# Turning the output projection on VectorE instead of folding it with an fp32 product, in a kernel of two attentions

## The chip, the cores and the metric

The kernel runs on one core of a Trainium2 chip. Its five engines have queues of their own: TensorE (PE in the profile; its weight loads are PEld), VectorE (DVE), ScalarE (ACT), GpSimd (POOL) and SyncE (SP), which here issues nearly all DMAs. They wait for each other by semaphores. The metric is the device time of one execution in microseconds; the median of several runs is compared.

## The reference, cut to what matters

Two attentions read the same input `x` (2048 tokens of 512), and a gate mixes them. Attention A is a recurrence over 64 segments of 32 tokens; each segment's input is 8 memory rows and its 32 tokens, and the first 8 rows of its output are the next segment's memory:

```python
g = sigmoid((x * gate_w).sum(-1, keepdims=True))
mem = mem0                                    # 8 rows of 512
for s in range(64):
    h = concatenate([mem, x[:, 32*s:32*s+32]])            # 40 rows
    q, k, v = h @ Wq, h @ Wk, h @ Wv                      # 32 heads of 128
    scores = where(mask, q @ k.T * scale, -1e9)           # memory rows see all keys, tokens causally
    o = (softmax(scores) @ v) @ Wo                        # back to 512, summed over the heads
    mem, out_a[s] = o[:8], o[8:]
# attention B: 32 heads of 16, four stretches of 512 tokens,
# causal softmax inside a stretch and a linear memory over the earlier ones
out = g * out_a + (1 - g) * out_b
```

All inputs are bf16.

## The kernel before, in words

**The two strands.** A's 64 segments (`p_seg`) are a chain: segment s+1 can't project before segment s has made its memory. B is cut into 16 units (`p_unit`: a stretch and 8 heads each), whose products fill TensorE's time while a segment waits. A third kind of filler are the "remainders": the last 8 tokens of each segment do not depend on the memory for their own projections, so `p_rest` projects those of four segments together, and a segment's own products have 32 rows (24 tokens and 8 memory rows).

**A segment.** The inputs of the projections are in `hT` (two buffers, 128 partitions x 4 chunks x 32 columns): 24 columns of tokens are copied from `xT` by GpSimd (L1441), 8 columns of memory come from the segment before. `wproj` (L1401) multiplies them with Wq, Wk and Wv, each product cut into four strips of 32 columns of the array (mode `c32`), four matmuls side by side. The results are copied out of PSUM to `st` (`copy`, L1001, on ScalarE or VectorE), transposed on VectorE to `KT` and `QT` (L1466), and multiplied to scores: first the mask as a product of `neg` and `hide` (`f_hide`, through `mm`, L1024), then the own scores (L1481) and those of the remainder's keys (L1485). ScalarE takes the exponential to `PT` (L1489); `ones` times `PT` gives the sums (L1504), ScalarE makes their reciprocal `rc` with a logarithm and an exponential (L1508, L1510), VectorE and GpSimd multiply `PT` with it (L1512, L1515), and TensorE multiplies with V (L1546, L1555, cut into strips of 32 rows, mode `r32`). The results are copied to `OT` (L1001), and `wo` multiplies them with Wo.

**`wo`.** 64 products a segment (L1300) leave four partial sums in one PSUM bank: partitions 0 to 63 hold the even heads, 64 to 127 the odd ones, and of each 64 the first 32 hold output columns 0 to 255 and the others 256 to 511, tokens along the partitions. The next segment needs the sum of the two halves, for the 8 memory rows, with the 512 columns along the partitions. The kernel before copies the bank to `part` in fp32 (name `par`), and multiplies each 128 columns of it with a fixed fp32 matrix `fold` of 16 columns, which picks the memory rows, adds the halves and turns the result (`f_fold`, through `mm`, L1024, in `c32`); VectorE copies the 32 columns to `hT` (name `hm`, L1323). The rows for the output are added from PSUM and `part` (name `row`, L1330) and go to DRAM (`a_rows`), from where `p_tail` reads them, scales them with the gate (L1275), adds B (L1283) and stores.

**B.** A piece of a unit is up to 16 `r32` products (L1141), two exponentials of 640 columns (L1159) and a causal select on GpSimd (L1165); pieces ride on a segment's PSUM banks (`carry`) or stand alone. Products with V are L1182, their transposes on VectorE L1218 and L1234. The gate itself is 64 products of one column (`f_gate`, L934), 16 for each 512 tokens.

**The start.** 16 MB of Wq, Wk, Wv and Wo are loaded in order by SP (`p_weight`, L897); before them come x and B's three projections (L806, 512 KB each), and small things, mem0 among them (L804).

**The order.** Every operation has a cost and a priority, and a planner (`schedule`) places operations on engines, modes and PSUM banks; but the sequence of each engine is not searched at build time: it is given by the text `ORDER`, which `sequences` unpacks. Costs only decide the engine's internal books. Each engine executes its sequence in that order and waits where a semaphore asks for it.

## Time and profile before

| | us |
|---|---|
| median of 3 runs | 830.68 (829.51 to 831.47) |
| profiled execution | 832.89 |
| its span, first to last instruction | 831.2 |
| TensorE busy | 809.5 (97%) |
| VectorE busy | 617.3 (74%) |
| ScalarE busy | 562.9 (68%) |
| GpSimd busy | 260.9 (31%) |
| granted TensorE clock | 0.998 |

Busy time counts any moment in which an instruction of the engine is under way. A matmul's record covers its way through the array, so that records overlap, and their sum says little; the chain of waits follows the work that ended last, from each step back to what released it, and gives every moment of the span to one step. Groups of instructions are listed as line, engine, operation, out<-in, shapes, count, then busy us, mean ns of one, and the engine's idle time just before them with what ended it.

### The profile page before, as it was taken

The numbers are of one execution on the slowest core, as the hardware profiler recorded it, in microseconds if no ns is written. First come the engines' busy times: TensorE is split into PE (matmuls) and PEld (weight loads), VectorE is DVE, ScalarE is ACT, GpSimd is POOL, SyncE is SP. The second block draws the span as 40 slices with busy tenths as digits, with TensorE's granted clock in tenths as the row PEclk, the third lists the DMA queues.
The fourth block names the chain that finished last, engine by engine and source line by source line (L and its number), as shares of the span: only waits on it lengthen the run. The fifth ranks groups of instructions, "written<-read, shape, count | busy, mean of one in ns | idle before, by whom it ended". The sixth has DMA issues, their size and how long they took to land.

```text
span 831.2 us, 53272 instructions
## 1 busy us (share of the span) xinstructions
PE 809.5 (97%) x24474; PEld 521.5 (63%) x24474; DVE 617.3 (74%) x1398; ACT 562.9 (68%) x1278; POOL 260.9 (31%) x576
## 2 busy tenths in 40 slices
PE   9999999999999999999999999999999999999987
PEld 4445666666666566666666666666766665666654
DVE  4688667768778768678676687776878767886776
ACT  3577676777766667776667766676656677767663
POOL 3443231323322332323233233423232223323340
PEclk9999999999999999999999999999999999999999
DMA  9983111121111111111011111100111100000001
GB/s 341 414 247 52 40 24 43 43 45 27 43 28 28 39 28 44 27 34 44 15 47 46 38 27 31 40 14 18 44 42 32 39 20 15 13 23 23 22 21 36
DMA packets 71701, 45.63 MB, mean 55 GB/s; under 512 B 50046, under 2 KB 69942, under 8 KB 69942
## 3 DMA queue, kind: packets, MB, share of 16 engines
q1 hardware_dynamic: 70422, 41.18, 17.5%
q8 instruction: 192, 3.15, 1.6%
...
q14 instruction: 31, 0.25, 0.1%
...
## 4 chain that ended last, share of the span: by engine, by line
PE 87%; DVE 4%; ACT 3%; DMA 2%; issue 1%; SPq 1%; POOL 0%; DVEq 0%; POOLq 0%
PE pb L1401 47%; PE pb L1300 17%; PE pb L1024 7%; PE pb L1141 4%; PE pb L1026 2%; PE pb L1546 2%; PE pb L1182 2%; DMA st<-in_A_mem_dram 2%; PE pb L1504 2%; PE pb L1481 1%; PE pb L1230 1%; PE pb L1555 1%; DVE KT_sb L1466 1%; PE pb L1485 1%; ACT rc_sb L1510 1%
## 5 line engine op out<-in xcount | busy, mean ns | idle before, releaser
L1001 ACT ACTIVATE st<-pb 128x512 bf16<-128x512 f32 (+2 forms) x313 | 149.0, 494 | 103.0 <-PE pb L1401 78.0
L1159 ACT ACTIVATE PTB<-pb 128x640 bf16<-128x640 f32 x240 | 158.4, 703 | 37.2 <-PE pb L1141 32.5
L1401 PE MATMUL pb<-Wv_sb,hT 128*32 128x512 bf16 x2048 | 162.8, 381 | 0.2 <-DVE ao L1330 0.2
L1401 PE MATMUL pb<-Wq_sb,hT 128*32 128x256 bf16 (+1 forms) x3072 | 138.0, 308 | 0.1
L1300 PE MATMUL pb<-Wo_sb,OT_sb 128*32 128x256 bf16 x4096 | 132.8, 273 | 3.0 <-issue 1.9
L1401 PE MATMUL pb<-Wk_sb,hT 128*32 128x512 bf16 x2048 | 132.0, 379 | 0.1
L1300 PEld LDWEIGHTS pb<-Wo_sb,OT_sb 128*32 128x32 bf16 x4096 | 100.7, 96 | 18.4 <-ACT OT_sb L1001 4.3
L1165 POOL TENSOR_SCALAR_AFFINE_SELECT PTB<-PTB 128x512 bf16<-128x512 bf16 x120 | 77.6, 647 | 107.4 <-ACT PTB L1159 100.8
L1515 POOL TENSOR_TENSOR PT_sb<-PT_sb,rc_sb 128x64 bf16<-128x64 bf16 x90 | 33.1, 367 | 248.9 <-ACT rc_sb L1510 240.5
L1401 PEld LDWEIGHTS pb<-Wq_sb,hT 128*32 128x32 bf16 x3072 | 82.5, 97 | 39.1 <-issue 0.8
L1466 DVE STREAM_TRANSPOSE QT_sb<-st 128x256 bf16<-128x256 bf16 (+1 forms) x192 | 94.4, 510 | 16.7 <-ACT st L1001 15.1
L1466 DVE STREAM_TRANSPOSE KT_sb<-st 128x512 bf16<-128x512 bf16 x128 | 89.4, 700 | 11.6 <-ACT st L1001 9.5
L1001 ACT ACTIVATE OT_sb<-pb 128x320 bf16<-128x320 f32 (+1 forms) x140 | 58.1, 428 | 37.9 <-PE pb L1555 36.3
L1401 PEld LDWEIGHTS pb<-Wk_sb,hT 128*32 128x32 bf16 x2048 | 57.0, 97 | 42.4 <-ACT PTB L1159 1.1
L1001 DVE CAST OT_sb<-pb 128x320 bf16<-128x320 f32 (+1 forms) x120 | 56.8, 478 | 31.3 <-PE pb L1555 29.3
L1401 PEld LDWEIGHTS pb<-Wv_sb,hT 128*32 128x32 bf16 x2048 | 52.2, 98 | 18.8 <-DVE ao L1330 0.7
L1508 ACT ACTIVATE rc_sb<-pb 128x160 f32<-128x160 f32 x128 | 38.8, 303 | 36.3 <-PE pb L1504 35.3
L1323 DVE CAST hT<-pb 128x32 bf16<-128x32 f32 x63 | 12.0, 191 | 66.4 <-PE pb L1024 66.1
L1489 ACT ACTIVATE PT_sb<-pb 128x224 bf16<-128x224 f32 x128 | 45.6, 356 | 17.4 <-PE pb L1485 12.8
L1001 DVE CAST V_sb<-pb 128x512 bf16<-128x512 f32 x65 | 44.5, 685 | 9.9 <-PE pb L1401 9.0
L1512 DVE TENSOR_TENSOR PT_sb<-PT_sb,rc_sb 128x160 bf16<-128x160 bf16 x128 | 42.7, 334 | 8.2 <-ACT rc_sb L1510 6.7
L1001 ACT ACTIVATE stg<-pb 128x512 bf16<-128x512 f32 (+1 forms) x68 | 37.9, 559 | 14.3 <-PE pb L1401 10.2
...
## 6 DMA issues: line engine op xcount, KB each, us to landing
...
```

Source lines behind the costliest of these rows:

```text
L1001: self.P.op(("act", "dve"), (lambda a: a.activation(dst, src(), ACT.Copy), lambda d: d.tensor_copy(dst, src())), reads=reads, writes=write ...
L1024: ins = pe.matmul(out[32 * c:32 * c + 32], lhsT[:, 32 * c:32 * c + 32], rhs, start=start, stop=stop, tile_position=(0, 32 * c), **kw)
L1141: ins = pe.matmul(pb[slot.banks[i]][:, base + a - lo:base + b - lo], KT[r0:r1, 128 * kc:128 * kc + 128], Q[r0:r1, t0 + a:t0 + b], start=Tr ...
L1159: P.op("act", (lambda dst=dst, src=src: lambda a: a.activation(dst, src(), ACT.Exp, scale=0.25))(), reads=[pair], writes=["%s%d_%d" % (nam ...
L1165: P.op("gp", (lambda pt=pt, ii=ii: (lambda g: g.affine_select(pt, pt, ([[0, len(ii)]] if len(ii) > 1 else []) + [[1, 128]], ALU.is_ge, 0.0 ...
L1300: ins = pe.matmul(pb[so.b][p0:p0 + 32, 0:256], tok(r, g, l), self.Wo[:, h, 256 * d:256 * d + 256], start=(r == 0 and g == 0 and l < 2), st ...
L1401: ins = pe.matmul(self.pb[sl.b][32 * g:32 * g + 32, 0:hi - lo], x[:, c, 0:32], cols, start=(c == 0), stop=(c == C - 1), tile_position=(0, ...
L1466: op("dve", (lambda dst=dst, src=src: lambda d: d.transpose(dst, src))(), reads=["st%d%s" % (i, tag)], writes=["%sT%d%s" % (kind, r, tag)] ...
L1489: op("act", lambda a: a.activation(PT[:, r, :], pb[rb.b][:, 0:224], ACT.Exp, scale=SCALE), reads=[rb], writes=["PT%d" % r, "PT%dr" % r], n ...
L1508: op("act", lambda a: a.activation(rc[:, r, :], pb[rb.b][:, 0:160], ACT.Ln), reads=[rb], writes=[rr], name="ln%d_%d" % (s, r), cost=t_act( ...
L1512: op("dve", lambda d: d.tensor_tensor(PT[:, r, 0:160], PT[:, r, 0:160], rc[:, r, :], ALU.mult), reads=[rp, rr], writes=[rp], name="nrm%d_% ...
L1515: op(("dve", "gp"), tuple((lambda e: e.tensor_tensor(rest, rest, late(rc[:, r, :]), ALU.mult)) for _ in range(2)), reads=[rp + "r", rr], w ...
```

## The change

- `wo`: the product with `fold` and the copy to `hT` go. VectorE transposes the PSUM bank's 256 fp32 columns in blocks of 32x32 to `rc` (`turn`), ScalarE or GpSimd moves the upper 64 partitions' memory columns to the lower 64 (`shift`), and two adds, on VectorE or GpSimd, put the sums of 64 partitions each into `hT` (`hm`). So that the blocks land where `hT` wants them, the products with Wo take 32 columns out of every 64 (`half`), and `p_tail` puts the columns back in order when it scales. The copy `par` is of the upper 64 partitions alone and has a later priority.
- The score bank is four pieces of 56 columns, 16 for the remainder and 40 of its own, instead of 160 and 64; the mask covers 40 of each, 160 columns instead of 224. What reads or writes scores and `PT` follows.
- The gate is made by 64 products of 128 columns in four column strips, with a transpose on VectorE behind each 16.
- B's first loads are of 384 columns instead of 512; the rest of them was not used from there.
- Costs and latencies of the planner are changed, and `ORDER` is new: all engines' sequences differ, the DMAs' too. In SP's, mem0 comes first.

The diff, without the two order texts, most changed costs and some renamings:

```diff
--- before
+++ after
@@ -13,71 +13,72 @@
 ORDER = (
...
@@ -658,7 +659,7 @@
         self.gB, self.omgB = self.rc[:, 1, 0:32], self.rc[:, 1, 32:64]
-        self.hide = t("hide_sb", [128, 224])
+        self.hide = t("hide_sb", [128, 160])
...
@@ -803,8 +803,8 @@
         for k in "kqv":
-            dma(self.g_wB[k], (lambda k: lambda s: s.dma_start(self.wB[k], self.B_w[k].rearrange("(c p) n -> p c n", p=128)))(k),
-                writes=["wB" + k], name="dma_wB" + k, prio=-102 if k == "k" else -99, load=dict(k=3.0, q=2.0, v=1.5)[k], cost=0.5, ring=4.0,
+            dma(self.g_wB[k], (lambda k: lambda s: s.dma_start(self.wB[k][:, :, 0:384], self.B_w[k].rearrange("(c p) n -> p c n", p=128)[:, :, 0:384]))(k),
+                writes=["wB" + k], name="dma_wB" + k, prio=-102 if k == "k" else -99, load=dict(k=2.7, q=1.6, v=1.15)[k], cost=0.5, ring=4.0,
...
@@ -820,9 +820,6 @@
         op("dve", lambda g: g.memset(self.MZf[:, :], 0.0), writes=["MZ16"], name="mz1", cost=0.15, prio=small)
-        for d in range(2):
-            op("dve", lambda v, d=d: v.tensor_tensor(self.fold[:, 8 * d:8 * d + 8], ident[:, 32 * d + 24:32 * d + 32], ident[:, 32 * d + 88:32 * d + 96],
-                                                     ALU.add), reads=["ident"], writes=["fold"], name="fold", cost=0.2, prio=small)
...
@@ -846,7 +843,8 @@
             op("dve", (lambda tile=tile: lambda g: g.memset(tile[:], 0.0))(), writes=[name], name=name + "0", cost=0.15, prio=small)
-        hide = [("hide", self.hide[0:32, lo:hi].rearrange("p (h q) -> p h q", h=4)) for lo, hi in ((0, 160), (160, 224))]
+        hide = self.hide[0:32, :].rearrange("p (h q) -> p h q", h=4)
+        hide = [("hide", hide[:, :, lo:hi]) for lo, hi in ((16, 40), (0, 16))]
...
@@ -929,14 +927,18 @@
             ins = None
-            for i in range(4):
-                for c in range(C):
-                    ins = pe.matmul(pb[sg.b][:, i:i + 1], xT[:, c, i * 128:(i + 1) * 128], self.gw[:, c:c + 1], start=(c == 0), stop=(c == C - 1))
+            for c in range(C):
+                part = xT[:, c, :].rearrange("p (i b t) -> p b i t", i=4, b=4)
+                for b in range(4):
+                    ins = pe.matmul(pb[sg.b][32 * b:32 * b + 32, 0:128], self.gw[:, c, :], part[:, b], start=(c == 0), stop=(c == C - 1),
+                                    tile_position=(0, 32 * b))
             return ins
-        P.op("pe", f_gate, reads=self.xres(sb) + ["gw"], writes=[sg], name="gate%d" % sb, cost=0.45, prio=prio + 0.1)
+        P.op("pe", f_gate, reads=self.xres(sb) + ["gw"], writes=[sg], name="gate%d" % sb, cost=0.23, prio=prio + 0.1, mode="c32")
         gs = self.g[:, 4 * sb:4 * sb + 4]
         rg, ro = "g%d" % sb, "omg%d" % sb
-        P.op("act", lambda a: a.activation(gs, pb[sg.b][:, 0:4], ACT.Exp, scale=-1.0), reads=[sg], writes=[rg], name="gate_e%d" % sb,
+        flat = self.adot[:, 0:8, :].rearrange("p a b -> p (a b)")
+        P.op("dve", lambda d: d.transpose(flat, pb[sg.b][:, 0:128]), reads=[sg], writes=["adot"], name="gate_t%d" % sb, cost=0.27, prio=prio + 0.1)
+        P.op("act", lambda a: a.activation(gs, flat.rearrange("p (i t) -> p i t", t=32)[:, :, 0], ACT.Exp, scale=-1.0), reads=["adot"], writes=[rg], name="gate_e%d" % sb,
...
@@ -1272,7 +1274,8 @@
               reads=["ad%d_%d" % (t, k) for k in range(n // 32)], writes=[ra], name="ain%d" % t, cost=0.4, load=0.2, prio=prio - 0.2)
-        P.op("dve", lambda d: d.tensor_scalar(self.t1[0:n, :], ain[0:n, :], self.g[0:n, t:t + 1], None, op0=ALU.mult),
+        P.op("dve", lambda d: d.tensor_scalar(self.t1[0:n, :].rearrange("p (m d i) -> p m d i", d=2, i=32), ain[0:n, :].rearrange("p (d m i) -> p m d i", d=2, i=32),
+                                             self.g[0:n, t:t + 1], None, op0=ALU.mult),
...
@@ -1289,6 +1292,11 @@
         so = P.slot("F", parts=True)
+
+        def half(h, d):
+            w = self.Wo[:, h, :]
+            return w[:, 256 * d:256 * d + 256] if late is None else w.rearrange("p (m d i) -> p d m i", d=2, i=32)[:, d]
+
...
@@ -1297,7 +1305,7 @@
                             p0 = 64 * q + 32 * d
-                            ins = pe.matmul(pb[so.b][p0:p0 + 32, 0:256], tok(r, g, l), self.Wo[:, h, 256 * d:256 * d + 256], start=(r == 0 and g == 0 and l < 2),
+                            ins = pe.matmul(pb[so.b][p0:p0 + 32, 0:256], tok(r, g, l), half(h, d), start=(r == 0 and g == 0 and l < 2),
...
@@ -1312,23 +1320,23 @@
         rhl = list(rhl) if isinstance(rhl, tuple) else [rhl]
-        self.copy(part, lambda: pb[so.b][:, 0:256], 256, [so], rhl, "par%s" % name, prio)
         if mem:
-            def f_fold(pe, m):
-                ins = None
-                for c in range(2):
-                    ins = self.mm(pe, m, pb[so.b][:, 256 + 16 * c:272 + 16 * c], part[:, 128 * c:128 * c + 128], self.fold[:, :], True, True)
-                return ins
-            P.op("pe", f_fold, reads=rhl + ["fold"], writes=[so], name="fold%s" % name, cost=0.15, prio=prio, mode=("c32",))
-            P.op("dve", lambda d: d.tensor_copy(mem[0].rearrange("p (d c) t -> p d c t", d=2),
-                                                pb[so.b][:, 256:288].rearrange("p (c d t) -> p d c t", c=2, d=2)), reads=[so], writes=[mem[1]],
-                 name="hm%s" % name, cost=0.19, prio=prio)
+            flat = self.rc[:, :, :].rearrange("p r x -> p (r x)")[:, 0:256]
+            turned = flat.rearrange("p (c e t) -> p e c t", c=4, e=2)
+            P.op("dve", lambda d: d.transpose(flat, pb[so.b][:, 0:256]), reads=[so], writes=["rc0", "rc1"], name="turn%s" % name, cost=0.43, prio=prio)
+            shift = self.rc[:, :, :].rearrange("p r x -> p (r x)")[0:64, 256:320].rearrange("p (e c t) -> p e c t", c=4, e=2)
+            P.op(("act", "gp"), ((lambda a: a.activation(shift, turned[64:128, :, :, 24:32], ACT.Copy)), (lambda g: g.tensor_copy(shift, turned[64:128, :, :, 24:32]))),
+                 reads=["rc0", "rc1"], writes=["rcs"], name="shift%s" % name, cost=(0.26, 0.26), prio=prio)
+            for e in range(2):
+                P.op(("dve", "gp"), tuple((lambda v, e=e: v.tensor_tensor(mem[0][64 * e:64 * e + 64], turned[0:64, e, :, 24:32], shift[:, e], ALU.add)) for _ in range(2)),
+                     reads=["rc0", "rc1", "rcs"], writes=["%s%d" % (mem[1], e)], name="hm%s_%d" % (name, e), cost=(0.16, 0.28), prio=prio)
+        self.copy(part[64:128, :], lambda: pb[so.b][64:128, 0:256], 256, [so], rhl, "par%s" % name, prio + 0.2 if mem else prio)
         i = self.__dict__.setdefault("nrow", [0])
         b = i[0] % 2
         i[0] += 1
         ao, rao = self.ao[b], "ao%d" % b
         P.op("dve", lambda d: d.tensor_tensor(ao[:, :], pb[so.b][0:64, 0:256], part[64:128, :], ALU.add), reads=[so] + rhl, writes=[rao],
-             name="row%s" % name, cost=0.45, prio=late)
+             name="row%s" % name, cost=0.42, prio=late)
...
@@ -1436,10 +1444,15 @@
             return P.slot("A")
+
+        def by_head(t):
+            return t.rearrange("p (l q) -> p l q", l=4)
+
+        mine, rest = [by_head(PT[:, r, :])[:, :, 16:56] for r in range(2)], [by_head(PT[:, r, :])[:, :, 0:16] for r in range(2)]
         xcol = (s % 16) * SEG
         xT = self.xT[sb % 2]
         op("gp", lambda g: g.tensor_copy(hv[:, :, 0:24], xT[:, :, xcol:xcol + 24]), reads=self.xres(sb, s % 16 // 4), writes=[rx],
-           name="hx%d" % s, cost=0.34, prio=s - 1)
+           name="hx%d" % s, cost=0.3, prio=s - 1)
...
@@ -1471,18 +1484,18 @@
             def f_hide(pe, m):
-                return self.mm(pe, m, pb[rb.b][:, 0:224], self.neg[:, :], self.hide[:, :], True, True, skip_group_check=True)
-            op("pe", f_hide, reads=["neg", "hide", "st%d" % i], writes=[rb], name="H%d_%d" % (s, r), cost=0.1, prio=prio, mode=FLEX)
+                return self.mm(pe, m, by_head(pb[rb.b][:, 0:224])[:, :, 0:40], self.neg[:, :], self.hide[:, :].rearrange("p (h q) -> p h q", h=4), True, True, skip_group_check=True)
+            op("pe", f_hide, reads=["neg", "hide", "st%d" % i], writes=[rb], name="H%d_%d" % (s, r), cost=0.072, prio=prio, mode=FLEX)
 
             def f_sc(pe):
                 ins = None
                 for l in range(4):
                     for g in range(4):
-                        ins = pe.matmul(pb[rb.b][32 * g:32 * g + 32, l * L:(l + 1) * L], KT[:, 16 * r + 4 * g + l, :], QT[:, 16 * r + 4 * g + l, :],
+                        ins = pe.matmul(pb[rb.b][32 * g:32 * g + 32, 56 * l + 16:56 * l + 56], KT[:, 16 * r + 4 * g + l, :], QT[:, 16 * r + 4 * g + l, :],
                                         start=False, stop=True, tile_position=(0, 32 * g), skip_group_check=True)
                 for g in range(4):
                     h0 = 16 * r + 4 * g
-                    ins = pe.matmul(pb[rb.b][32 * g:32 * g + 32, 160:224], Kr[:, h0:h0 + 4].rearrange("p h k -> p (h k)"), QT[:, h0:h0 + 4, 24:40],
+                    ins = pe.matmul(by_head(pb[rb.b][32 * g:32 * g + 32, 0:224])[:, :, 0:16], Kr[:, h0:h0 + 4].rearrange("p h k -> p (h k)"), QT[:, h0:h0 + 4, 24:40],
...
@@ -1500,7 +1513,7 @@
                     o = pb[rb.b][p0:p0 + n]
-                    for k, (dst, src) in enumerate(((o[:, 0:160], PT[:, r, 0:160]), (late(o[:, 0:160]), PT[:, r, 160:224]))):
+                    for k, (dst, src) in enumerate(((by_head(o[:, 0:160]), mine[r]), (late(o[:, 0:160]), rest[r]))):
...
@@ -1509,11 +1522,10 @@
                cost=0.335, prio=prio)
-            op("dve", lambda d: d.tensor_tensor(PT[:, r, 0:160], PT[:, r, 0:160], rc[:, r, :], ALU.mult), reads=[rp, rr],
-               writes=[rp], name="nrm%d_%d" % (s, r), cost=0.335, prio=prio)
-            rest = PT[:, r, 160:224].rearrange("p (l q) -> p l q", q=16)
-            op(("dve", "gp"), tuple((lambda e: e.tensor_tensor(rest, rest, late(rc[:, r, :]), ALU.mult)) for _ in range(2)), reads=[rp + "r", rr],
-               writes=[rp + "r"], name="nrr%d_%d" % (s, r), cost=(0.235, 0.33), prio=prio)
+            op("dve", lambda d: d.tensor_tensor(mine[r], mine[r], by_head(rc[:, r, :]), ALU.mult), reads=[rp, rr],
+               writes=[rp], name="nrm%d_%d" % (s, r), cost=0.345, prio=prio)
+            op(("dve", "gp"), tuple((lambda e: e.tensor_tensor(rest[r], rest[r], late(rc[:, r, :]), ALU.mult)) for _ in range(2)), reads=[rp + "r", rr],
+               writes=[rp + "r"], name="nrr%d_%d" % (s, r), cost=(0.3, 0.38), prio=prio)
...
@@ -1552,11 +1564,11 @@
                     o = pb[quad.banks[g]][:, 0:160].rearrange("p (l q) -> p l q", q=L)[:, :, 24:40]
-                    ins = pe.matmul(o, Vr[p0:p0 + 32, 128 * r:128 * r + 128], PT[p0:p0 + 32, r, 160:224],
+                    ins = pe.matmul(o, Vr[p0:p0 + 32, 128 * r:128 * r + 128], rest[r][p0:p0 + 32],
                                     start=False, stop=True, tile_position=(p0, 0), skip_group_check=True)
                 return ins
-            op("pe", f_pv, reads=["V%d" % r, "PT%d" % r], writes=quad.pairs + (self.early(3) if s == 0 else []), name="PV%d_%d" % (s, r), cost=0.11, prio=pPV[r], mode="r32")
-            op("pe", f_pw, reads=["PT%dr" % r, rVr[r]], writes=quad.pairs, name="PW%d_%d" % (s, r), cost=0.035, prio=pPV[r], mode="r32")
+            op("pe", f_pv, reads=["V%d" % r, "PT%d" % r], writes=quad.pairs + (self.early(3) if s == 0 else []), name="PV%d_%d" % (s, r), cost=0.088, prio=pPV[r], mode="r32")
+            op("pe", f_pw, reads=["PT%dr" % r, rVr[r]], writes=quad.pairs, name="PW%d_%d" % (s, r), cost=0.06, prio=pPV[r], mode="r32")
...
```

160 lines of the change are left out of this document (80 added, 80 removed).

## The prediction

> **What bounds the kernel now.** I read the page first: the engines' shares, then the chain that ended last.
>
> ```profile
> span 831.2 us, 53272 instructions
> PE 809.5 (97%) x24474; PEld 521.5 (63%) x24474; DVE 617.3 (74%) x1398; ACT 562.9 (68%) x1278; POOL 260.9 (31%) x576
> PE 87%; DVE 4%; ACT 3%; DMA 2%; issue 1%; SPq 1%; POOL 0%; DVEq 0%; POOLq 0%
> PE pb L1401 47%; PE pb L1300 17%; PE pb L1024 7%; PE pb L1141 4%; PE pb L1026 2%; PE pb L1546 2%; PE pb L1182 2%; DMA st<-in_A_mem_dram 2%; PE pb L1504 2%; PE pb L1481 1%; PE pb L1230 1%; PE pb L1555 1%; DVE KT_sb L1466 1%; PE pb L1485 1%; ACT rc_sb L1510 1%
> ```
>
> TensorE carries 87% of the chain and VectorE only 4%: what leaves TensorE's queue is worth nearly its own length, and what is added to VectorE is free as long as it ends before TensorE asks for it. TensorE's own length must not be read from the durations of single products, because these overlap. The chain between 400 and 430 us, one steady stretch of two to three segments, gives what each kind takes of the path (start, us, what):
>
> ```profile
> 404.79 0.43 PE pb L1401 x8
> 405.22 0.11 PE pb L1024 x16
> 405.58 4.01 PE pb L1401 x88
> 409.59 0.10 PE pb L1024 x4
> 409.68 0.22 PE pb L1401 x4
> 410.00 0.04 PE pb L1485 x4
> 411.00 0.10 PE pb L1504 x8
> 414.72 0.04 PE pb L1555 x4
> 417.48 0.11 PE pb L1024 x16
> ```
>
> Four 512-column products, one for each 32-column strip of the array, take 0.22 us together: 0.43 ns a column of such a set. There is no idle time to speak of between rows. The x16 rows of L1024 are the fp32 products (fold, eight products that the trace records as sixteen); the x4 row at 409.59 is the 224-column mask.
>
> **Fold out of TensorE.** 63 segments have one. On the chain it costs 0.11 us: 63 x 0.11 = 6.9 us, the lower end. The group that holds all of them, and the weight loads of the same product:
>
> ```profile
> L1024 PE MATMUL pb<-fold_sb,st 128*32 128x16 f32 x1008 | 19.9, 186 | 1.6 <-ACT st L1001 1.2
> L1024 PEld LDWEIGHTS pb<-fold_sb,st 128*32 128x32 f32 x1008 | 16.0, 110 | 13.4 <-ACT st L1001 8.7 <-DVE st L1001 1.9 <-issue 0.4
> ```
>
> 19.9 us of busy time is the upper end. The Trainium skill (Trainium Kernel Development and Optimization, Performance Expectations) says that busy time of matmuls is a bad measure because they are pipelined; these rows agree, 186 ns for one against 0.11 us for sixteen; by the rule the 19.9 is left aside, by busy time the sum below would be 11.4 us better. I take the chain's 6.9 and the 1.6 us that TensorE stood idle in front of fold: 8.5 us off.
>
> **What replaces it.** The old way from Wo's last product to the next segment's memory columns, once in full:
>
> ```profile
> 404.40 0.42 DVE L1001 COPY st<-pb 128x256 f32<-128x256 f32 x1 [2.50 <-PE pb L1300]
> 404.88 0.35 PEld L1024 LDWEIGHTS pb<-fold_sb,st 128*32 128x32 f32 x16 [0.16 <-DVE st L1001]
> 405.05 0.28 PE L1024 MATMUL pb<-fold_sb,st 128*32 128x16 f32 x16
> 405.43 0.19 DVE L1323 CAST hT<-pb 128x32 bf16<-128x32 f32 x1 [0.60 <-PE pb L1024]
> 405.68 0.60 PEld L1401 LDWEIGHTS pb<-Wq_sb,hT 128*32 128x32 bf16 x16
> ```
>
> From the copy's start to the first projection: 405.68 - 404.40 = 1.28 us. The new way has a 128x256 fp32 transpose out of PSUM, a 64x64 move of the upper partitions to the lower (48 on ScalarE, 15 on GpSimd in the new order), and two 64x32 adds, 115 of 126 on VectorE. None is in the trace; the nearest rows:
>
> ```profile
> L1466 DVE STREAM_TRANSPOSE QT_sb<-st 128x256 bf16<-128x256 bf16 x128 | 50.6, 415 | 4.1 <-ACT st L1001 3.4
> L1466 DVE STREAM_TRANSPOSE KT_sb<-st 128x512 bf16<-128x512 bf16 x128 | 89.4, 700 | 11.6 <-ACT st L1001 9.5
> L1218 DVE STREAM_TRANSPOSE t_sb<-pb 128x512 f32<-128x512 f32 x32 | 22.6, 706 | 2.5 <-PE pb L1182 2.5
> L939 ACT ACTIVATE g_sb<-pb 128x4 f32<-128x4 f32 x4 | 0.7, 173 | 0.5 <-PE pb L934 0.5
> L1508 ACT ACTIVATE rc_sb<-pb 128x160 f32<-128x160 f32 x128 | 38.8, 303 | 36.3 <-PE pb L1504 35.3
> L1108 DVE TENSOR_TENSOR MZ<-MZ,t_sb 128x17 f32<-128x17 f32 x12 | 2.0, 164 | 0.2
> L1515 DVE TENSOR_TENSOR PT_sb<-PT_sb,rc_sb 128x64 bf16<-128x64 bf16 x38 | 9.1, 240 | 2.2 <-ACT rc_sb L1510 1.8
> L1323 DVE CAST hT<-pb 128x32 bf16<-128x32 f32 x63 | 12.0, 191 | 66.4 <-PE pb L1024 66.1
> ```
>
> fp32 from PSUM costs a transpose nothing at 512 columns (706 against 700), so 0.42 us at 256. The move lies between 0.17 (4 columns) and 0.30 (160): 0.23. An add lies between 0.16 and 0.24: 0.18. A hand-over between engines is 0.06 (0.42 after 404.40, then 404.88). Quiet, the new way is 0.42 + 0.06 + 0.23 + 0.06 + 2 x 0.18 + 0.06 = 1.19 us (1.09 to 1.38 by the ends), against 1.28: no longer than the old one. It must be covered by products that need neither. I counted those between Wo's last product and the first projection in both instruction orders, at 0.43 ns a column: 1.17 us on average in the old, without fold, 1.24 in the new. Fold's own 0.11 was cover too, which makes 1.28 against 1.24. So the path gets hardly longer or barer, and I put this at 0; by the ends it is -0.19 + 0.04 = -0.15 to 0.10 + 0.04 = +0.14 us a segment, 9 us either way. An add that waits for the move holds up what the new order queues behind it on VectorE, the copy of the sums, the row's add and the next K and Q transposes, and the last of these wait for the projections anyway. The copy of the sums stays, on 64 partitions, and is put behind the memory columns, where only the row's way to DRAM waits for it.
>
> VectorE gains 63 x 0.42 + 115 x 0.18 - 12.0 = 35 us, and about 10 us of copies that the new order gives to it: 617 + 45 = 662 us, 81% of the new span. It stays below TensorE, with less slack for anything queued there.
>
> **Mask.** 64 columns fewer, 128 times (two a segment), at 0.43 ns: 3.5 us off; bounds 0 (if the x4 row's 0.10 were a floor) and 3.5. The price is a score bank in four pieces of 56, so that the mask, and the remainder's scores, are written in pieces. The softmax weights' products on VectorE and GpSimd read pieces too; they are off the path.
>
> **Gate.** Its 64 one-column products become 64 of 128 columns on four strips:
>
> ```profile
> L934 PE MATMUL pb<-gw_sb,xT 128*128 128x1 bf16 x64 | 2.2, 164 | 0.0
> L1401 PE MATMUL pb<-Wv_sb,hT 128*32 128x512 bf16 x2048 | 162.8, 381 | 0.2 <-DVE ao L1330 0.2
> L1401 PE MATMUL pb<-Wk_sb,hT 128*32 128x512 bf16 x2048 | 132.0, 379 | 0.1
> ```
>
> 2.2 us become 16 sets of 128 columns, 16 x 128 x 0.43 ns = 0.9 us: 1.3 off, with four small transposes beside it. Wo's weights are now read 32 columns out of every 64. That costs nothing: Wk is read in pieces of 32 already, Wv in one piece, 379 against 381 ns.
>
> **First loads.** Three of 512 KB lose a quarter, 384 KB in all, and mem0, on the chain with 14.39 us, goes to the head of SP's queue, past x, two of the three loads and Wv, which its 8 KB hardly delay.
>
> ```profile
> GB/s 341 414 247 52 40 24 43 43 45 27 43 28 28 39 28 44 27 34 44 15 47 46 38 27 31 40 14 18 44 42 32 39 20 15 13 23 23 22 21 36
> 7.18 14.39 DMA st<-in_A_mem_dram
> ```
>
> At 414 GB/s 384 KB are 0.9 us, by which the weights queued behind land earlier. The 14.39 us are no gain of that size: the first projection then waits for its weights, which come in that same stream. I take 0.9; bounds 0 and 3.
>
> **New order.** The other queues are shuffled throughout; in the two orders TensorE changes between products cut by rows and all others about equally often (372 and 370 times). I take 0. DVE, ACT, DMA, issue and SP hold 11% of the chain, 91 us; a tenth of it either way, 9 us, is the bound.
>
> **Sum.** 8.5 + 3.5 + 1.3 + 0.9 = 14.2 us off. The profiled execution took 832.9 us (its span and 1.7 us around it), 2.2 over the median of 830.7: 832.9 - 14.2 = 818.7 for its like, 816.5 for a median.
>
> **Rivals.** What a measurement of this kernel can tell from no change is about 0.2%, 1.7 us.
>
> (a) Fold's place becomes a wait. What counts for it: 13.4 us of idle weight loading stand ahead of fold, so TensorE does wait for this way today; the projection would wait in its stead. Then the 8.5 stay and 5.7 us go: 825.0.
>
> (b) The new order is better than the old by its bound, and takes another 9 us out of the 91: 807.5. For it: a little more cover (1.24 against 1.17); against it: nothing in the profile says that the remaining waits are needless.
>
> (c) Slower: the move waits on ScalarE. In the new order 44 of the 48 ScalarE moves stand right behind a half-unit exponential of
>
> ```profile
> L1159 ACT ACTIVATE PTB<-pb 128x640 bf16<-128x640 f32 x240 | 158.4, 703 | 37.2 <-PE pb L1141 32.5 <-DVE OT_sb L1001 3.2
> ```
>
> 0.70 us. One that starts with the transpose ends 0.28 us after it, one that starts at its end 0.70: 0.49 on average, and 44 x 0.49 = 21.6 us. That makes 816.5 + 21.6 = 838.1. It decides from 14.2 / 44 = 0.32 us a segment. Against it: ScalarE is idle 32% of the time, and the exponential may have run before Wo ends.
>
> (d) Writing in pieces slows the products: were the mask's 0.07 us (160 columns) and the remainder's 0.04 doubled, 128 x 0.11 = 14.1 us would come back and the time would be 830.6, no change. Against it: L1555 writes pieces of 16 out of 40 today and takes 0.04 us for four products of 64 columns, as L1485 does in one piece; that speaks plainly, so it gets little. The Trainium skill (SBUF — State Buffer, in the passage on cachelines under the DMA port swizzle) has the rule: any non-contiguous access to PSUM slows matmuls significantly. This trace disagrees at pieces of 16.
>
> **How the numbers follow.** Forecast 0.48; (a) 0.17; (b) 0.17; (c) 0.13; (d) 0.05. The likeliest gives 816.5, by its own bounds (9 us either way) 808 to 825. The range runs from 802 (a few us beyond b, since fold's true share may reach its upper end) to 831, which holds all but (c) and the far end of (b). Faster: forecast, a and b, 0.82, less a little for their tails: 0.80. Same: d, 0.05. Slower: c and tails, 0.15.
>
> **What would show it.** Right: no fp32 product in the groups, the mask's row at 0.07 us, TensorE's busy time down by some 14 us at the same 97%, VectorE near 81%, and the first projections of a segment released at about the old distance from Wo's end. Wrong: idle TensorE time in front of the projections put down to VectorE's adds or ScalarE's move (a, c), more than 0.04 us for the remainder's scores (d), or other waits that grew by more than 9 us in all.

## The result, and the profile after

The changed kernel takes 841.16 us (median of 4 runs, 840.17 to 842.98) against 831.08 us for the kernel before beside it (4 runs, 829.51 to 833.61): a ratio of 1.0121, 95% interval 1.009 to 1.0152. The forecast was 816.5 us, with a range from 802 to 831. The profiled execution took 840.17 us, with a span of 838.4.

The page of the changed kernel: its span, the engines' shares, and the chain that ended last, by engine and by line.

```profile
span 838.4 us, 51578 instructions
PE 804.2 (96%) x23514; PEld 497.5 (59%) x23514; DVE 669.8 (80%) x1556; ACT 565.5 (67%) x1286; POOL 269.2 (32%) x601
PE 73%; DVE 13%; ACT 4%; DMA 3%; issue 3%; SPq 2%; POOL 1%; DVEq 0%; POOLq 0%; ACTq 0%
PE pb L1409 40%; PE pb L1308 15%; PE pb L1026 5%; PE pb L1143 3%; PE pb L1558 2%; PE pb L1028 2%; PE pb L1184 2%; DVE rc_sb L1326 2%; DVE hT L1331 2%; PE pb L1494 2%; PE pb L1517 2%; DMA st<-in_gate_w_dram 1%; DVE stg L1003 1%; SPq L1381 1%; DVE ao L1338 1%
```

TensorE fell from 87% to 73% of the chain and VectorE rose from 4% to 13%. TensorE's busy time hardly moved (809.5 to 804.2 us); VectorE's grew by 52.5 us (617.3 to 669.8). The new operations are lines L1326 (turn), L1328 (move) and L1331 (adds). Groups of instructions, with mean duration in ns and the idle time ahead of them:

```profile
L1326 DVE STREAM_TRANSPOSE rc_sb<-pb 128x256 f32<-128x256 f32 x63 | 28.2, 448 | 45.0 <-PE pb L1308 44.6
L1328 ACT ACTIVATE rc_sb<-rc_sb 64x64 f32<-64x64 f32 x48 | 12.2, 254 | 26.5 <-DVE rc_sb L1326 26.1
L1331 DVE TENSOR_TENSOR hT<-rc_sb 64x32 bf16<-64x32 f32 x115 | 26.5, 231 | 14.1 <-ACT rc_sb L1328 8.5 <-POOL rc_sb L1328 3.1
L1026 PE MATMUL pb<-hide_sb,neg_sb 128*32 128x160 bf16 x508 | 31.6, 233 | 0.1
L1498 PE MATMUL pb<-QT_sb,rem_k 128*32 128x64 bf16 x512 | 27.1, 196 | 0.0
```

Beside its 54.7 us of turns and adds, VectorE stands idle for 14.1 us in front of adds, mostly because the move isn't done: an engine works in its given order, and what is queued behind an add waits too. One such way in the timeline, with nothing in between:

```profile
592.69 0.45 DVE L1326 STREAM_TRANSPOSE rc_sb<-pb 128x256 f32<-128x256 f32 x1 [0.92 <-PE pb L1308]
593.18 0.26 ACT L1328 ACTIVATE rc_sb<-rc_sb 64x64 f32<-64x64 f32 x1 [0.31 <-DVE rc_sb L1326]
593.47 0.40 DVE L1331 TENSOR_TENSOR hT<-rc_sb 64x32 bf16<-64x32 f32 x2 [0.32 <-ACT rc_sb L1328]
593.92 0.34 PEld L1409 LDWEIGHTS pb<-Wq_sb,hT 128*32 128x32 bf16 x12
```

From turn to projection that is 1.23 us, close to the 1.19 forecast. TensorE now waits for the adds and, for its PSUM banks, for the rows' adds (waits: us in total, times, longest):

```profile
PEld pb L1409 <- DVE hT L1331: 15.4, 32, 1.2
PE pb L1409 <- DVE hT L1331: 6.5, 20, 0.7
PEld pb L1409 <- DVE ao L1338: 5.8, 15, 1.0
```

In the kernel before, the same pairs stand at 1.1 us (hT) and 0.9 us (ao) on weight loading. Not all of the 15.4 us is new: there TensorE waited in front of fold instead, with the 13.4 us of idle weight loading that the prediction shows.

### The profile page after: what moved, and what is told of

It reads as the page before. It is cut to its first block, busy times and chain, and to the rows that moved or that the text cites. A ratio compares the mean times of both kernels' runs of the same rounds, so it can differ in the third digit from the quotient of the medians.

```text
span 838.4 us, 51578 instructions
## 1 busy us (share of the span) xinstructions
PE 804.2 (96%) x23514; PEld 497.5 (59%) x23514; DVE 669.8 (80%) x1556; ACT 565.5 (67%) x1286; POOL 269.2 (32%) x601
## 4 chain that ended last, share of the span: by engine, by line
PE 73%; DVE 13%; ACT 4%; DMA 3%; issue 3%; SPq 2%; POOL 1%; DVEq 0%; POOLq 0%; ACTq 0%
PE pb L1409 40%; PE pb L1308 15%; PE pb L1026 5%; PE pb L1143 3%; PE pb L1558 2%; PE pb L1028 2%; PE pb L1184 2%; DVE rc_sb L1326 2%; DVE hT L1331 2%; PE pb L1494 2%; PE pb L1517 2%; DMA st<-in_gate_w_dram 1%; DVE stg L1003 1%; SPq L1381 1%; DVE ao L1338 1%
## 5 line engine op out<-in xcount | busy, mean ns | idle before, releaser
L1003 ACT ACTIVATE st<-pb 128x512 bf16<-128x512 f32 (+2 forms) x286 | 140.0, 507 | 92.8 <-PE pb L1409 82.2
L1409 PE MATMUL pb<-Wv_sb,hT 128*32 128x512 bf16 x2048 | 158.4, 380 | 0.5 <-DVE QT L1001 0.3
L1308 PE MATMUL pb<-Wo_sb,OT_sb 128*32 128x256 bf16 x4096 | 136.2, 274 | 3.5 <-issue 2.3
L1308 PEld LDWEIGHTS pb<-Wo_sb,OT_sb 128*32 128x32 bf16 x4096 | 98.3, 96 | 24.0 <-ACT OT_sb L1003 4.8
L1409 PEld LDWEIGHTS pb<-Wq_sb,hT 128*32 128x32 bf16 x3072 | 79.9, 97 | 50.8 <-DVE hT L1331 4.9
L1479 DVE STREAM_TRANSPOSE KT_sb<-st 128x512 bf16<-128x512 bf16 x128 | 88.9, 697 | 15.2 <-ACT st L1003 13.4
L1003 ACT ACTIVATE OT_sb<-pb 128x320 bf16<-128x320 f32 (+2 forms) x133 | 54.8, 427 | 46.9 <-PE pb L1567 44.3
L1409 PEld LDWEIGHTS pb<-Wk_sb,hT 128*32 128x32 bf16 x2048 | 54.5, 96 | 53.6 <-DVE hT L1331 10.4
L1003 DVE CAST OT_sb<-pb 128x320 bf16<-128x320 f32 (+2 forms) x127 | 59.3, 478 | 24.0 <-PE pb L1567 23.0
L1326 DVE STREAM_TRANSPOSE rc_sb<-pb 128x256 f32<-128x256 f32 x63 | 28.2, 448 | 45.0 <-PE pb L1308 44.6
L1525 DVE TENSOR_TENSOR PT_sb<-PT_sb,rc_sb 128x160 bf16<-128x160 bf16 x128 | 42.8, 335 | 9.9 <-ACT rc_sb L1523 8.9
L1523 ACT ACTIVATE rc_sb<-rc_sb 128x160 f32<-128x160 f32 x128 | 43.0, 336 | 3.7 <-ACT rc_sb L1521 0.3
```

Of the source, the lines that this page charges most:

```text
L1003: self.P.op(("act", "dve"), (lambda a: a.activation(dst, src(), ACT.Copy), lambda d: d.tensor_copy(dst, src())), reads=reads, writes=write ...
L1308: ins = pe.matmul(pb[so.b][p0:p0 + 32, 0:256], tok(r, g, l), half(h, d), start=(r == 0 and g == 0 and l < 2), stop=(r == 1 and g == 3 and ...
L1326: P.op("dve", lambda d: d.transpose(flat, pb[so.b][:, 0:256]), reads=[so], writes=["rc0", "rc1"], name="turn%s" % name, cost=0.43, prio=prio)
L1409: ins = pe.matmul(self.pb[sl.b][32 * g:32 * g + 32, 0:hi - lo], x[:, c, 0:32], cols, start=(c == 0), stop=(c == C - 1), tile_position=(0, ...
L1479: op("dve", (lambda dst=dst, src=src: lambda d: d.transpose(dst, src))(), reads=["st%d%s" % (i, tag)], writes=["%sT%d%s" % (kind, r, tag)] ...
L1523: op("act", lambda a: a.activation(rc[:, r, :], rc[:, r, :], ACT.Exp, scale=-1.0), reads=[rr], writes=[rr], name="rc%d_%d" % (s, r), cost= ...
```

## The experiments

Four theories: the path (the way from Wo to the next segment's memory columns got longer), the order (the new sequences lose), the layout (operands in pieces are slow), and, from the second round on, VectorE's load (work on VectorE costs time wherever it stands). Names with b keep the old order, names with a the new one. Ratios are to the kernel before, run on the same chip, with a 95% interval in brackets; 0.1% is 0.83 us, and differences in us are worked out from the ratios. The kernels for which an operation had to be put into an order that was not made for it have it placed by hand, by the planned times.

### First round: which part of the change loses

**b_mask.** `ORDER` of before; mask, scores and loads of after.

> The kernel before, in its own order of instructions, with the 160-column mask, the new layout of the scores and the shorter first loads; the fold, the gate and the output rows stay as they were. Three theories for the 10.1 us that the whole change costs (841.2 against 831.1). Path: the turn, the move and the two adds are a longer way to the next segment's first operand than copy, fold and copy. Order: the edits are worth what they were thought to be, and the new order of the instructions loses more than that. Layout: operands read in pieces (scores, weighed values, Wo) are slower at TensorE or VectorE. Path and order expect 825 to 829 us here (3.5 us for the mask, 0.9 for the loads, up to 2 less); layout expects 835 us or more.

Measured: 829.78 us, ratio 0.9975 (0.995 to 0.9999). The layout does not lose; mask and loads bring about 2 us, only just clear of nothing. It is the fastest version here that computes everything, and the only one ahead of both kernels.

**b_turn.** The fold's part of `wo` is replaced as in the change's diff, with `half` for Wo; the rest is before.

> The kernel before, in its own order, with one edit: the fold and its two neighbours are replaced by the turn (at the old copy's time on VectorE), the move on ScalarE, the two adds on VectorE (right behind the move by the planned times) and the halved copy behind them; Wo is read in blocks of 32 columns with it. Every other instruction keeps its place. Path expects the whole loss here: 838 to 846 us. Order expects a gain or nothing: 822 to 831 us. Layout expects a small loss from Wo's pieces: 832 to 835 us.

Measured: 850.52 us, 1.0218 (1.0188 to 1.0249). The loss comes with the turn, and in the old order it is larger than the whole change's, and larger than path expected.

**a_fold.** The reverse: copy, fold and copy put into the changed kernel.

> The changed kernel in its own order, with the fold back: the turn, move and adds go; the copy of all 128 rows stands where the turn was (on the engine that had it in the kernel before), the fold is put on TensorE 0.62 us behind it by the planned times, and its copy on VectorE behind that. Mask, gate, loads and the order of all else are the changed kernel's. Path expects the loss gone: 826 to 832 us. Order expects it kept or grown, since the fold was fitted into this order by hand: 838 to 850 us.

Measured: 850.0 us, 1.0217 (1.0191 to 1.0242). Path expected the loss gone, and it grew. Taken with b_turn this decides nothing: each of the two operations was put by hand into an order that was made for the other, and both kernels are slow.

**b_all.** b_mask and b_turn together.

> The kernel before in its own order with the mask, the layout of the scores, the shorter loads and the turn together (all of the change but the gate's product and the new order). If the order alone loses: 819 to 828 us, the sum of the gains without the new order. If the path loses: 835 to 842 us, the path's loss less 4 us for mask and loads. Layout expects 838 us or more, and more than the turn alone.

Measured: 846.64 us, 1.0177 (1.0147 to 1.0207): b_turn less about 3.4 us, where mask and loads alone brought 2.1: the parts add up within their intervals. It is above the 835 to 842 that path expected, and layout, which expected more than for the turn alone, falls.

### Second round: path against load

**b_hm2.** Before, with `hm` (L1323) cut in two:

```diff
-P.op("dve", copy mem[0] <- pb[so.b][:, 256:288], name="hm")
+for e in range(2):
+    P.op("dve", copy mem[0][64*e:64*e+64] <- pb[so.b][64*e:64*e+64, 256:288], name="hm_e")
```

> The kernel before with one edit that makes its way from Wo to the next segment longer by a known piece and changes nothing else: the copy of the memory columns to hT is done in two halves of 64 partitions, one behind the other on VectorE, which adds about 0.19 + 0.03 = 0.22 us a segment to that way and 12 us of busy time to VectorE. Path theory (what counts is when the next segment's memory columns are ready): in the trace of before the projection starts some 0.09 us later than it could in the median segment, so that 0.13 to 0.22 us a segment come out at the end: 8 to 14 us, 839 to 845. Theory of VectorE's load: 12 us of 617 more, 831 to 834.

Measured: 838.57 us, 1.0092 (1.0068 to 1.0116), 7.6 us. The path theory holds for this edit: 63 x 0.22 = 13.9 us of path cost a little over half of that, just under the 8 to 14 expected. The second copy is VectorE work too, some 12 us.

**b_load.** Before, with two transposes whose results nobody reads:

```diff
 P.op("dve", ..., name="hm%s" % name)
+P.op("dve", transpose(spare, OT[:, 0:256]), name="duma%s" % name)
 P.op("dve", ..., name="row%s" % name)
+P.op("dve", transpose(spare, OT[:, 0:256]), name="dumb%s" % name)
```

> The kernel before with VectorE's load of the changed kernel and without its path: two transposes of 128x256 (0.42 us each, 52 us in all, as much as the change adds) whose results nobody reads, one right behind the copy of the memory columns, one right behind the output row's add. Path theory: 831 to 834 us, since both stand behind what the next segment waits for. Theory of VectorE's load (copies, transposes and sums that queue on a VectorE at 80% come late to TensorE): the loss comes here, 838 to 845 us.

Measured: 839.52 us, 1.0106 (1.0069 to 1.0143), 8.8 us. The load theory's case, off the path. The two groups, and the chain by engine:

```profile
L1334 DVE STREAM_TRANSPOSE spare<-OT_sb 128x256 bf16<-128x256 bf16 x63 | 28.1, 445 | 1.9
L1326 DVE STREAM_TRANSPOSE spare<-OT_sb 128x256 bf16<-128x256 bf16 x63 | 27.4, 435 | 0.1
PE 82%; DVE 8%; ACT 4%; DMA 3%; issue 2%; SPq 1%; POOL 0%; DVEq 0%; POOLq 0%
```

55.5 us of idle work on an engine that had 4% of the chain cost 8.8 us, 0.16 us each, and VectorE's share of the chain doubled. (The two rows add to 55.5 us, but the records of neighbours on VectorE overlap: its busy time on the page grew by 34.0 us, from 617.3 to 651.3, and by that the price is 0.26.) More waits of TensorE than before end with K's and Q's transposes and with the rows' adds:

```profile
PEld pb L1484 <- DVE QT_sb L1469: 7.2, 23, 0.7
PEld pb L1484 <- DVE KT_sb L1469: 4.9, 14, 0.5
PEld pb L1404 <- DVE ao L1331: 4.6, 16, 0.9
```

These were 4.1, 1.9 and 0.9 us.

**a_noshift.** The changed kernel without the move; `hm` adds `turned[0:64]` to itself.

> The changed kernel in its own order without the move between partitions: the two adds take the lower half twice, so the odd heads' half is left out of the memory rows. The way from Wo to hT is shorter by the move and its hand-over, 0.25 + 0.03 us quiet and more where it queues. Path theory: 841 less 63 x (0.15 to 0.28) = 9 to 18 us, 823 to 832 us. Theories of load and of order: only ScalarE has 12 us less to do, 838 to 841 us.

Measured: 836.12 us, 1.0054 (1.0034 to 1.0074), 5.6 us below the changed kernel by the ratios: more than load and order expected (none to 3 us), less than the 9 to 18 of the path. A shorter path alone does not bring the kernel back to 831. The edit also takes away the adds' wait for the move, so that VectorE stands idle for 3.1 us in front of them instead of 14.1.

**b_split.** Before, with the copy `par` cut in two halves of 128 columns, `st3` and `st3b`, one on each engine.

> The kernel before with its path made shorter: the copy of the four partial sums ahead of the fold is cut in two halves of 128 columns, one on ScalarE and one on VectorE, side by side. Each is about 0.12 us shorter than the whole (0.27 against 0.39), but the fold now waits for both engines to be free. Path theory: the same slope downwards, up to 63 x 0.12 = 7 us less, if neither queue is late: 824 to 831 us; where one of the two is late by more than 0.12 us on average, 831 to 838. Theory of load: 10 us more on VectorE and ScalarE together, 831 to 833 us.

Measured: 839.75 us, 1.0101 (1.008 to 1.0121). In none of the 63 segments did the halves run side by side; the kernel's own bookkeeping lets the readers of one PSUM bank follow each other:

```profile
306.76 0.29 DVE L999 COPY st<-pb 128x128 f32<-128x128 f32 x1 [0.73 <-PE pb L1298]
307.08 0.28 ACT L999 ACTIVATE st<-pb 128x128 f32<-128x128 f32 x1
307.41 0.22 PEld L1022 LDWEIGHTS pb<-fold_sb,st 128*32 128x32 f32 x16 [0.34 <-ACT st L999]
```

So the path got longer by about 0.2 us, and the run is a second b_hm2: nearly the same loss, a little above the 831 to 838 expected for late halves.

The records of each trace tell path from load: the time from the start of Wo's last product to the first projection with the new memory columns, summed over 63 segments, is 107.7 us in the kernel before, 115.0 in b_hm2, 116.5 in b_split and 107.4 in b_load. A longer path pays in this stretch, an idle load pays outside it. The changed kernel has 112.7, 5.0 more than before. b_turn has 123.1 and a_fold 122.9: both pay 15 of their 18 us there, a_fold with VectorE as little busy as before (620.8 us). So the path can cost much; b_load shows that it is not all that costs.

### Third round: order and load with the path taken out

All four kernels have `hT` filled by one copy straight from Wo's bank (the row `hT<-pb` below), and turn, move and adds off the path; fold's sum and turning are left out of the memory rows. "dload" has them in full size, "dlight" on 32 and 8 columns:

```diff
+P.op("dve", copy mem[0] <- pb[so.b][:, 0:32], name="hmx")
 turn, shift as before (dlight: flat[:, 0:32], shift[:, 0, 0:1])
-add -> mem[0][64*e:64*e+64]
+add -> spare[64*e:64*e+64]
```

**a_dlight.**

> The changed kernel in its own order, with the way to the next segment taken out of the question: hT gets 32 columns straight from Wo's bank by one copy of 0.19 us at the place of the turn (fold, turning and adding are left out of the memory rows), and turn, move and adds stand where they stood, but off the path (they write a scratch) and small: 32 columns turned, 8 columns moved and added. That leaves the new order of all else, with some 35 us less on VectorE than in the changed kernel. If path and VectorE's load are all that the change lost, the time falls below before's 831 by mask, gate and fold: 822 to 829 us. If the new order itself loses, it stays at 832 to 836 us.

**a_dload.**

> As the kernel with the small operations off the path, but turn, move and adds in their full size (into the scratch): VectorE has the changed kernel's whole load and 12 us more, and nothing of it is on the path. Theory of load: 5 us or more above the small one (the two idle transposes of before cost 7.6 us for 52 us of VectorE, 0.15 us each), 829 to 836 us. Path alone: equal to the small one within 2 us.

**b_dlight.**

> The same as the kernel with the small operations off the path, but in the order of the kernel before (with mask, layout of scores and shorter loads; the old gate): one direct copy to hT at the time of the old copy of the sums, small turn, move and adds into a scratch at the places that they had in the kernel with the turn in the old order. Against the same in the new order it tells what the order is worth with path and load out of the way. Order is innocent: within 3 us of it, 820 to 829 us. New order loses: 5 us or more below it. Against mask and loads alone (829.8) it shows what a free path and no fold are worth: by the prediction's fold term 8.5 us, 821.

**b_dload.**

> As the one before, in the order of the kernel before, with turn, move and adds in full size into the scratch. Theory of load: 5 us or more above the small one. Path alone: equal to it within 2 us, and far below the 846.6 of the same order with these on the path.

| | new order | old order |
|---|---|---|
| small | 831.36 us, 1.0011 (1.0001 to 1.002) | 830.64 us, 1.0016 (0.9999 to 1.0034) |
| full size | 839.40 us, 1.0104 (1.0087 to 1.012) | 839.45 us, 1.0115 (1.0097 to 1.0133) |
| full size, on the path | 841.16 us, 1.0121 (the changed kernel) | 846.64 us, 1.0177 (b_all) |

The columns agree in the first two rows: the order is innocent (the new one has the new gate beside it, forecast at 1.3 us). Each step downwards: size costs 7.7 us in the new order and 8.2 in the old, putting it on the path 1.4 and 5.1. That the new order hides the longer path better would fit, but is not shown: the intervals do not tell 1.4 from 5.1. The last step also drops the direct copy, 11.9 us of VectorE, so that it shows a little less than what the path costs. For size, the theory of load held; the times themselves, 822 to 829 us for the small kernel in the new order, 820 to 829 in the old, and 829 to 836 for a_dload, were all missed from above. The groups of a_dlight, then of a_dload, say why:

```profile
L1324 DVE CAST hT<-pb 128x32 bf16<-128x32 f32 x63 | 11.9, 189 | 42.7 <-PE pb L1308 42.3
L1333 DVE TENSOR_TENSOR spare<-rc_sb 64x8 bf16<-64x8 f32 x115 | 24.8, 216 | 12.5 <-ACT rc_sb L1330 7.1 <-POOL rc_sb L1330 2.7
L1328 DVE STREAM_TRANSPOSE rc_sb<-pb 128x32 f32<-128x32 f32 x63 | 12.9, 205 | 0.0
```

```profile
L1333 DVE TENSOR_TENSOR spare<-rc_sb 64x32 bf16<-64x32 f32 x115 | 25.5, 221 | 13.9 <-ACT rc_sb L1330 8.4 <-POOL rc_sb L1330 3.0
L1328 DVE STREAM_TRANSPOSE rc_sb<-pb 128x256 f32<-128x256 f32 x63 | 27.7, 439 | 0.0
L1330 ACT ACTIVATE rc_sb<-rc_sb 64x64 f32<-64x64 f32 x48 | 12.2, 254 | 28.9 <-DVE rc_sb L1328 28.8
PE 70%; DVE 16%; ACT 5%; issue 3%; DMA 3%; POOL 2%; SPq 1%; DVEq 0%; ACTq 0%; POOLq 0%
```

An add of 8 columns is on average nearly as long as one of 32, and VectorE waits for the move in front of it as before. The "small" kernel still held VectorE for 12.9 + 24.8 + 12.5 = 50 us; it was not the kernel without load that it was meant to be. Nor is all of the load VectorE's: in a_dload the moves on ScalarE take 12.2 us, and it stands idle for 28.9 us in front of them.

### Fourth round: what the removed work was worth

**a_direct.** a_dlight without turn, move and adds.

> The changed kernel in its own order with the direct copy from Wo's bank to hT alone: turn, move and adds are gone (fold, turning and adding are left out of the memory rows). Against the same with the small operations off the path (831.4), VectorE has some 20 us less to do and ScalarE 8. If VectorE's load costs 0.15 to 0.25 us for each of its us down to there: 826 to 829 us. If the load only costs above a threshold: 830 to 832 us.

Measured: 824.89 us, 0.9916 (0.9893 to 0.9939), just below the 826 to 829 expected. So the load costs from the start and not only above a threshold: 7.9 us up to the small operations, 7.7 more up to the full ones. It is not in proportion: the first step is the 50 us above, the second 14.8 us of turn, 0.7 of adds and 1.4 of waiting. Mask, gate, loads, the removed fold and the short path together bring 7.0 us once nothing replaces the fold.

```profile
PE 793.9 (96%) x23498; PEld 498.6 (61%) x23514; DVE 632.5 (77%) x1441; ACT 552.1 (67%) x1238; POOL 262.1 (32%) x575
PE 82%; ACT 5%; DVE 4%; issue 2%; DMA 2%; POOL 2%; SPq 2%; DVEq 0%; ACTq 0%; POOLq 0%
```

VectorE is back at 4% of the chain. How long TensorE's weight loads wait goes the same way: put down to VectorE, it is 42.8 us in a_direct, 50.5 in a_dlight, 59.3 in a_dload and 66.1 in the changed kernel; put down to ScalarE, 47.6, 51.6, 51.4 and 49.3.

The stretch from Wo to the projection is 99.4 us in a_direct, 98.5 in a_dload and 112.7 in the changed kernel. So a_dload pays for the new operations wholly outside that stretch, and the changed kernel pays 13.3 us of them inside: taken off the path, the loss moves and does not go away.

**b_tiny.** Before, with fold as one product of one column:

```diff
-for c in range(2):
-    ins = self.mm(pe, m, pb[so.b][:, 256 + 16*c:272 + 16*c], part[:, 128*c:128*c + 128], self.fold, True, True)
+ins = pe.matmul(pb[so.b][0:32, 256:257], self.ident[:, 0:32], self.ident[:, 0:1], True, True)
```

> The kernel before in its own order; fold is one product of a single column that waits for nothing but Wo, and the copy to hT takes 32 columns straight from Wo's bank (the sum of the halves and the turning are left out of the memory rows). Every other operation, VectorE's load among them, stays. So both terms of fold are gone: TensorE's time for it, 0.11 us a segment on the chain, and the way of copy, fold and copy. By the prediction's term: 8.5 us less than before, 822 to 824 us, and more if the shorter path brings something by itself. If TensorE's removed work only turns into waits: 828 to 832 us.

Measured: 828.63 us, 0.9962 (0.9941 to 0.9984), 3.2 us less. It did not do all that was expected of it: the product writes the bank that the copy reads, and so it still waits for the copy:

```profile
L1317 PEld LDWEIGHTS pb<-ident 128*32 128x32 bf16 x63 | 5.9, 93 | 13.3 <-ACT st L999 8.4 <-DVE st L999 1.7 <-ACT stg L999 0.7
```

The 13.4 us of idle weight loading in front of fold are still there. So 3.2 us (1.3 to 4.9) is the worth of fold's products, and of what they add to the path (the median way from Wo's end to the last write of `hT` falls from 1.11 to 0.99 us), not of the wait.

**b_mask2.** Before, with the mask's product issued twice.

> The kernel before with the 224-column mask product done twice, nothing else. TensorE has 128 x 224 columns more at 0.43 ns, 12.3 us. If TensorE's queue is the bound as the prediction took it (87% of the chain): 10 to 13 us more, 841 to 844. If its work is for the most part beside waits for VectorE and ScalarE: 3 to 6 us more, 834 to 837.

Measured: 852.36 us, 1.0255 (1.0212 to 1.0298): 21 us for 12.3 us of columns, above both expectations. TensorE's work is not hidden at all in the middle of a segment. Part of what it costs above its columns is waiting for which the profile names no cause ("issue"): in front of products it grew from 4.2 us in all to 9.8, in front of weight loads from 29.2 to 37.8. Why stays open; 504 more products came with 504 more weight loads, and a_quart below has a lead.

**b_loadrow.** b_load with `dumb` alone.

> The kernel before with one idle transpose of 128x256 a segment on VectorE, behind the output row's add, half of what cost 7.6 us with a second one right behind the memory columns' copy. If every us on VectorE costs the same wherever it stands: 26 us more load, 4 us, 835 to 836. If the place right in front of the K and Q transposes is what costs: 831 to 833.

Measured: 836.99 us, 1.0069 (1.0049 to 1.009), 5.7 us for 28.1 us of VectorE, 0.20 us each (0.31 by VectorE's busy time, which grew by 18.4 us). The place in front of K's and Q's transposes is not what costs.

### Last round: another engine pays

**a_addgp.** The changed kernel with `hm%s_1` of every segment on GpSimd where neither add was.

> The changed kernel in its own order with one of the two adds of each segment on GpSimd (64 in all instead of 11), put behind the move by the planned times; the other stays on VectorE. The whole result is computed. VectorE has some 12 us less, GpSimd 15 us more, and the two adds run side by side, so that the path is 0.1 us shorter where GpSimd is free. Theory of load (0.2 to 0.3 us for each us on VectorE): 841 less 3 us for the load, 2 for the path, 835 to 839 us. If GpSimd's queue (selects of 0.65 us) makes the add late: 841 to 846 us.

Measured: 842.75 us, 1.0123 (1.0087 to 1.0159), no different from the changed kernel. The add is late there:

```profile
L1330 POOL TENSOR_TENSOR hT<-rc_sb 64x32 bf16<-64x32 f32 x64 | 16.9, 265 | 52.1 <-ACT rc_sb L1327 48.2 <-POOL OTr_sb L1585 0.2
L1330 DVE TENSOR_TENSOR hT<-rc_sb 64x32 bf16<-64x32 f32 x62 | 13.8, 222 | 12.5 <-ACT rc_sb L1327 8.5 <-POOL rc_sb L1327 3.1
```

GpSimd waits 48 us for the moves, with its own queue behind it, and VectorE's wait has hardly shrunk (14.1 to 12.5 us). The stretch from Wo to the projection grew from 112.7 to 118.5 us, and the rest shrank by 3.3.

**a_quart.** Wo on four column strips of 128 columns, no move and no adds:

```diff
-for d in range(2): pe.matmul(pb[so.b][p0:p0 + 32, 0:256], tok, half(h, d), ...)
+for j in range(4): pe.matmul(pb[so.b][32*j:32*j + 32, 0:128], tok, Wo[:, h] (b j i -> j b i)[:, j], start=(h == 0), stop=(h == 31), ...)
+turned = transpose(pb[so.b][:, 0:128]);  mem[0] = turned[:, :, 24:32];  ao = copy(pb[so.b][:, 0:128])
```

> A version with neither fold, move nor adds that computes the whole result: the products with Wo go to four column strips of 128 output columns each, all 32 heads summed in one bank (128 products of 128 columns a segment instead of 64 of 256, the same time in columns). Then one transpose of 128x128 and one copy of the memory columns make hT, the output rows are one copy, and the copy of the sums goes. The changed kernel's order, mask and gate. VectorE has some 55 us less than in the changed kernel, the path is 0.4 us shorter. If TensorE takes twice the products in the same time (the gate's 128-column products run at 14 ns each in the trace after): 820 to 828 us. If the number of instructions binds (16,000 more with their weight loads, on 47,000): 850 us or more.

Measured: 919.2 us, 1.1047 (1.1016 to 1.1078). The number of instructions was misstated there: it is 4,032 more products and as many weight loads, 8,064 in all. That is enough (the last two lines are the page's rows of instruction packets, here and then in the changed kernel, with count, MB and share):

```profile
L1305 PE MATMUL pb<-Wo_sb,OT_sb 128*32 128x128 bf16 x8064 | 145.9, 220 | 53.3 <-issue 52.1
L1305 PEld LDWEIGHTS pb<-Wo_sb,OT_sb 128*32 128x32 bf16 x8064 | 119.8, 97 | 72.8 <-issue 59.5
PE 813.2 (89%) x27530; PEld 531.7 (58%) x27546; DVE 621.5 (68%) x1466; ACT 541.4 (59%) x1213; POOL 260.4 (28%) x575
q8 instruction: 216, 3.54, 1.6%
q8 instruction: 185, 3.03, 1.5%
```

TensorE stands idle in Wo for nothing that the profile names, and the gain of a VectorE at 68% is lost many times over. The products themselves are not slower: one follows the other at 14.5 ns, where those of 256 columns take 26.9. Over the whole kernel TensorE's products wait 79.1 us put down to "issue", against 3.4 in the changed kernel. The DMA records have a lead to the cause: all 67 of these stops that are longer than 0.3 us, 76.4 us together, end 1.2 to 1.6 us after a packet of the queue `q8 instruction` has ended, where only about a tenth of the kernel's time lies; so do all 12 such stops in b_mask2. That TensorE waits there for its own instructions is the likeliest reading, and no run tests it.

## Why the prediction was wrong

**The step that failed: VectorE's work was put at nothing.** Its amount was forecast well (662 us and 81%; it is 669.8 and 80%). Its price was not: "what is added to VectorE is free as long as it ends before TensorE asks for it", and "It stays below TensorE, with less slack for anything queued there". From a_direct to the changed kernel, that is from no replacement of fold to the whole one, the ratio goes from 0.9916 to 1.0121: 17.0 us for what the prediction put at 0. With nothing of it on the path it still costs 15.6 (a_dload), so no path, however well covered, would have made it free. The bound of 9 us either way was for the path alone; no case had a price for the load. A chain share of 4% says how long the path of one execution runs over VectorE. It doesn't say how far VectorE's other work is from being on it: b_load took it to 8% with work that nobody waits for.

What the 17.0 us consist of is less clear. The idle transposes' 0.16 to 0.20 us for each us would make 8.5 to 10.6 us of the 53.2 us of turn and adds in a_dload (an estimate from b_load and b_loadrow); the rest may be the waiting of VectorE and ScalarE for each other around the move, which no run takes alone. And load and path are not two terms that add: 1.4 us are left when the turn comes onto the path, although the stretch from Wo to the projection then grows by 14.2.

**The path.** It was put at 0, and this failed too. The quiet way was sized right (1.19 forecast, 1.23 in one case), but the medians of the traces are not quiet: from the start of copy or turn to the first weight load of the projection 1.24 us before and 1.37 after, from the end of Wo's last product to the last write of `hT` 1.11 and 1.35. By the second it is 0.24 us longer instead of 0.09 shorter, beyond the 0.14 of the bounds. The old way's 1.28 was one segment, close to that median. What this costs in the changed kernel is 5.0 us by the stretch from Wo to the projection, against the kernel before, which is inside the 9 us that were allowed. So rival (a), that the projection waits in fold's stead, happened (the 15.4 and 6.5 us above), but by its price the time would have been 825, not 841.

**Fold, 8.5 us.** Its products were worth 3.2 (1.3 to 4.9). The chain's 0.11 us a segment came from two segments of one stretch, and the 1.6 us of idle time could not be had, since the wait itself is part of the path.

**Mask and first loads, 3.5 and 0.9 us.** 2.1 measured together (0.1 to 4.2). The mechanism is right (the group fell from 259 to 233 ns), the size is within the bounds given. **Gate, 1.3.** Not run alone; a_direct's 7.0 less 3.2 and 2.1 leaves 1.7 for it, for the wait in front of fold and for the direct copy's short path, with VectorE 15 us busier than before.

**New order, 0.** Right as a forecast for the rest of the work (1.0011 against 1.0016, 1.0104 against 1.0115), so rival (b), an order better by 9 us, fell.

**Rival (c)** came near the time, 838.1, by another mechanism. The move hardly waits for an exponential: it starts 0.06 us after the turn's end on average, and ScalarE waits for the turn, 26.1 us of idle time in the row of L1328. **Rival (d)** fell by the sign that was named for it: on the chain between 400 and 430 us of the changed kernel the remainder's four products take 0.04 us and the mask's 0.07. b_mask, which writes the same pieces, does not lose either.

Of the other signs named, the fp32 products are gone and VectorE is at 80%. TensorE's busy time fell by 5.3 us instead of 14, and the idle time put down to VectorE's adds is there, as the text said it would be if wrong.

Summed: mask and loads -2.1, fold -3.2, the rest of a_direct's gain -1.7, what replaces fold +17.0: +10.0 us, against +10.1 measured. The sum closes because it is made of two differences that meet in a_direct; it is no proof of its own. Each term has an interval of about 2 us or more either way.
